# Window attention, forward and backward: two quads in one attention region, with three half sums a pair

## The chip, the cores and the metric

The kernel runs on one NeuronCore of a Trainium2 chip. The metric is the device time of one execution in microseconds. Every product runs on TensorE (PE), which writes PSUM, eight banks of 2 KB per partition; VectorE (DVE) and ScalarE (ACT) copy PSUM to SBUF and do the softmax; SyncE (SP) and GpSimd (POOL) issue the DMAs.

## The reference

The image has 256 x 256 positions and 384 channels in bf16, cut into 1024 windows of 8 x 8 positions. For each window, attention with one head, and then its gradients for a given `grad_out`:

```python
qkv = xw @ wqkv                      # xw: 64 tokens x 384 of one window
q, k, v = split(qkv)
p = softmax(q @ k.T * 384 ** -0.5)
o = (p @ v) @ wo
...
_out, _vjp = jax.vjp(_f, x, wqkv, wo)
return (out, *_vjp(grad_out))        # out, dx, dwqkv, dwo
```

The outputs are `out_0` = o and `out_1` = dx (both 256 x 256 x 384), `out_2` = dwqkv and `out_3` = dwo.

## The kernel before

**Products folded.** At the start the kernel builds A = wq wk' x scale and B = wv wo, and their transposes, 384 x 384 each. A window then needs only z (from grad_out by B', `project` kind 0), y (from x by A, kind 1), u (x by B) and v (x by A', `uv`), and not q, k and v by themselves. The weight gradients come at the end from two 384 x 384 sums over all windows, U'x and W'x, which are gathered in `GF_acc`.

**Tiling.** A *quad* is four pairs of windows: 8 windows, 512 tokens, a tile of 128 partitions x 4 x 384. There are 128 quads, numbered from 0. Quad i passes through: DMA loads of `xq` and `dq` (`load`, L133); their DMA transposes `xT` and `dT` (`load_turn`, L141); z and y into `yz` (`project`, L161); copies into `zy` (`gather`, L175, DVE) and a DMA transpose into `tok` (`to_tokens`, L181); scores into one PSUM bank `sd` (`scores`, L186: P's logits in one half of the partitions and their gradient in the other); the softmax and its gradient (`soft`, steps 0 to 5, DVE except for the exponential); transposes of the two 64 x 64 blocks on DVE (`turn`); u and v (`uv`, L233); and attention (`attend`, L268, once for each of the four window pairs).

**Two forms of matmul.** z, y, u, v, the scores and the row sums use the whole 128 x 128 array, through `product` (all recorded on L157). `attend` works in four tiles of 64 x 64: each `slot` (L277, its products recorded on L283) is four products of 64 rows, for `pw`, `pu`, `po` and `pd`, and the banks go out by `W` (ACT), `U` (DVE), `o` (ACT) and `d` (ACT or DVE, by the table `EV`).

**Sums for the weight gradients.** Three finished quads form a group (GQ = 3). Each group gives six pieces of work (2 sums x 3 row blocks), kept in `fill`. A piece is done in one of two forms: `gf_rows`, 12 products of 128 x 384 into one bank `pg` and one add into `GF_acc`; or `gf_halves`, 12 slots of four 64 x 64-tile products into two banks `ph` and two adds, the second after the first (L320).

**The order of the work** is written out by hand; each engine runs its queue in that order. `step` (L360) handles three quads at once: c (attention), b (scores, softmax, u, v) and a (z, y of the next). Its PE order is: scores of b; u and v of b; z and y of a; one row sum; then `attention` of c, where each of the four `attend` calls is followed by four slots of one half sum until its twelve are done. One row sum and one half sum a quad use up six pieces in three quads.

**PSUM.** All banks come from one pool `ring` of eight. A new tile gets a bank that the program has given back, and its first product waits for the copy (or add) that emptied it.

Of the kernel before, what the change touches and what calls it, by code (L numbers as in the profile page):

```python
# [11 lines left out]
BF16 = mybir.dt.bfloat16  # L12
F32 = mybir.dt.float32

P = 128
WIN = 8
WT = WIN * WIN
QUAD = 4
# [5 lines left out]
def kernel(  # L24
# [21 lines left out]
    nc = tc.nc  # L46
    _, H, W, C = x.shape
    CK = C // P
# [5 lines left out]
    grp = ctx.enter_context(tc.tile_pool(name="grp", bufs=2 * GQ + 1))  # L54
    qp = ctx.enter_context(tc.tile_pool(name="qp", bufs=2))
# [64 lines left out]
    OTHER = {0: HI, WT: LO}  # L120

    def load_first(st):
        st["xq"] = xq = grp.tile([P, QUAD, C], BF16, tag="xq", name="xq", bufs=2 * GQ + 5)
# [9 lines left out]
    def load(st):  # L133
        st["xq"] = xq = grp.tile([P, QUAD, C], BF16, tag="xq", name="xq", bufs=2 * GQ + 5)
        st["dq"] = dq = qp.tile([P, QUAD, C], BF16, tag="dq", name="dq", bufs=6)
        for t in range(QUAD):
            nc.gpsimd.dma_start(out=dq[:, t, :], in_=windows(grad_out, st, 2 * t))  # L137
        for t in range(QUAD):
            (nc.gpsimd if st["i"] == AHEAD + 1 else nc.sync).dma_start(out=xq[:, t, :], in_=windows(x, st, 2 * t))

    def load_turn(st):  # L141
        st["xT"] = qp.tile([P, QUAD, CK, P], BF16, tag="xT", name="xT", bufs=3)
        st["dT"] = qp.tile([P, QUAD, CK, P], BF16, tag="dT", name="dT")
        for src, dst, on_pe in (("dq", "dT", G_ON_PE), ("xq", "xT", X_ON_PE)):
            if st["i"] >= on_pe:
                nc.sync.dma_start_transpose(out=st[dst][:].rearrange("p t m k -> p (t m) k"),
                                            in_=st[src][:].rearrange("p t c -> p (t c)"))

    def turn_on_pe(st, src, dst):
        for t in range(QUAD):  # L150
# [117 lines left out]
    def attend(st, t):  # L268
        if t == 0:
            st["Uq"] = grp.tile([P, QUAD, C], BF16, tag="Uq", name="Uq")  # L270
            st["Wq"] = grp.tile([P, QUAD, C], BF16, tag="Wq", name="Wq")
        copies = {"A": nc.scalar.copy, "D": nc.vector.tensor_copy}

        def bank(name):
            return ring.tile([P, C], F32, tag="r", name=name)

        def slot(bank, straight, crossed, start=False, stop=False):  # L277
            for h in (LO, HI):
                o = OTHER[h.start]
                products = [(h, bank, straight, {"start": True, "stop": True}),  # L280
                            (o, pd[h is LO], crossed, {"start": start, "stop": stop})]
                for o, dst, (lhs, rhs), flags in products if h == LO else products[::-1]:
                    nc.tensor.matmul(dst[o, :], lhsT=operand(st, lhs, t, h), rhs=operand(st, rhs, t, h), **flags)  # L283

        def keep(name, src, i, rows=slice(0, P), sb=None):
            sb = ob.tile([P, C], BF16, tag=name, name=name) if sb is None else sb
            copies[EV[name][i]](out=sb[rows, :], in_=src[rows, :])  # L287
# [6 lines left out]
        copies[EV["W"][t] if st["i"] >= GQ else "DA"[t % 2]](out=st["Wq"][:, t, :], in_=pw[:])  # L294
        pu = bank("pu")
        slot(pu, ("ST", "xq"), ("dS", "y"))
        copies[EV["U"][t]](out=st["Uq"][:, t, :], in_=pu[:])  # L297
        po = bank("po")
        slot(po, ("PT", "uq"), ("ST", "vq"), stop=True)
        o = keep("o", po, t)  # L300
        above, below = rim.pop("d", None) if t == 0 else None, st["at"][0] + 2 * WIN * QUAD < H
        d = keep("d", pd[1], t, slice(0 if t else WT, P), above)
        nc.gpsimd.dma_start(out=windows(out_0, st, 2 * t), in_=o)  # L303
        if t or above is not None:
            nc.gpsimd.dma_start(out=windows(out_1, st, 2 * t - 1), in_=d if t else above[:])  # L305
        else:
            nc.gpsimd.dma_start(out=windows(out_1, st, 0, 1), in_=d)
        if t == QUAD - 1:
            rim["d"] = sb = ob.tile([P, C], BF16, tag="d", name="d")
            keep("d", pd[0], QUAD, LO, sb)  # L310
            if not below:
                nc.gpsimd.dma_start(out=windows(out_1, st, 2 * QUAD - 1, 1), in_=rim.pop("d")[LO, :])

    fill, rim = [], {}
# [34 lines left out]
                nc.vector.tensor_copy(out=final[f][:, ma, :], in_=GF_acc[:, f, ma, :])  # L349
                yield  # L350

    def attention(st):
        halves = gf_halves(*fill.pop(0)) if fill else iter(())
        for t in range(QUAD):
            attend(st, t)
            yield
            for k in range(QUAD):
                next(halves, None)

    def step(c, b, a, ahead):  # L360

# [40 lines left out]
        for rest in slots:  # L402
            pass

    G_ON_PE, X_ON_PE = 2, 1
    EV = {"z": "AAA", "y": "AAA", "u": "AAAA", "v": "AAAA", "o": "AAAA", "U": "DDDD", "W": "AAAA", "d": "DADAA"}
    quads = [(row, col) for col in range(0, W, WIN) for row in range(0, H, 2 * WIN * QUAD)]
    n = len(quads)
    sts = [{"at": q, "i": i, "on_pe": i <= GQ or i == n - 1} for i, q in enumerate(quads)]
# [4 lines left out]
    def weight_gradients(group):  # L414
# [19 lines left out]
                copy_out(k, out, pe[:])  # L434

        def rows(name):
            return grp.tile([P, CK, C], BF16, tag="xq", name=name, bufs=2 * GQ + 5)

        for i in range(CK):
            next(group)  # L440
# [26 lines left out]
    with tc.manual_schedule(engines=MANUAL):  # L467
        spare = sm.tile([P, 1], BF16, name="spare", bufs=1)
        fetch_weights()
        warm_up(7)  # L470
        make_identity(nc, ident[:])
        nc.gpsimd.memset(GF_acc[:], 0.0)
        load_first(sts[0])
        load(sts[1])
        load(sts[2])
        load_turn(sts[0])
        load_turn(sts[1])
# [19 lines left out]
        last = None  # L497
        get = lambda i: sts[i] if 0 <= i < n else None
        for i in range(n + 1):
            if 0 <= i < n - 2:  # L500
                load_turn(sts[i + 2])
            if 0 <= i < n:
                to_tokens(sts[i])
            step(get(i - 1), get(i), get(i + 1), get(i + AHEAD) if i else None)
            if i > 0:
                held.append(sts[i - 1])
                sts[i - 1] = None
            if held and i == n:
                last = gf_final(held)
            elif len(held) == GQ:  # L510
                fill.extend((held, f, ma) for f in range(2) for ma in range(CK))
                held = []
        while fill:
            gf_rows(*fill.pop(0))
        weight_gradients(last)
# [30 lines left out]
```

## Time and profile before

| what | value |
|---|---|
| median of 3 runs | 1897.86 us (1897.47 to 1898.12) |
| the profiled execution | 1897.33 us, of which its span 1895.6 us |
| granted TensorE clock | 1.00 from 300 to 1800 us |
| PE busy from 300 to 1800 us | 1500.00 of 1500.00 us |
| DVE, ACT, POOL busy in that time | 1334.00, 1218.28, 691.54 us |
| u and v products, z, y | 333.6 + 333.4, 269.6, 269.5 us |
| row sums pg, half sums ph | 181.6 + 94.8, 204.2 + 103.4 us |
| adds into GF_acc from ph, from pg | 138.1 us (250, 552 ns each), 74.1 us (133) |
| DMA transposes, median to landing | xT 7.7, dT 7.7, tok 7.4 us |

The span runs from the first to the last instruction of the profiled execution; the rest of its time lies around it. Matmuls are pipelined: an instruction lasts longer than the distance to the next one, so distances between starts are what counts. The same holds for copies on DVE and ACT.

### The profile page before, as it was taken

The numbers are of one execution on the slowest core, as the hardware profiler recorded it, in microseconds if no ns is written. First come the engines' busy times: TensorE is split into PE (matmuls) and PEld (weight loads), VectorE is DVE, ScalarE is ACT, GpSimd is POOL, SyncE is SP. The second block draws the span as 40 slices with busy tenths as digits, with TensorE's granted clock in tenths as the row PEclk, the third lists the DMA queues.
The fourth block names the chain that finished last, engine by engine and source line by source line (L and its number), as shares of the span: only waits on it lengthen the run. The fifth ranks groups of instructions, "written<-read, shape, count | busy, mean of one in ns | idle before, by whom it ended". The sixth has DMA issues, their size and how long they took to land.

```text
span 1895.6 us, 57194 instructions
## 1 busy us (share of the span) xinstructions
PE 1887.7 (100%) x22398; PEld 1125.4 (59%) x22398; DVE 1662.8 (88%) x3602; ACT 1523.7 (80%) x3346; POOL 862.6 (46%) x1576
## 2 busy tenths in 40 slices
PE   9999999999999999999999999999999999999999
PEld 5555565556555655565556555655565566556655
DVE  6888888888888888888888888888888888888887
ACT  7888788878887888788878887888788878887884
POOL 4444444445444444454445444544444445444532
PEclk9999999999999999999999999999999999999999
DMA  9999999999999999999999999999999999999995
GB/s 224 244 212 225 221 211 221 216 221 218 210 222 220 212 224 213 224 215 215 227 215 220 213 218 223 218 208 222 218 222 218 214 222 219 212 213 227 219 183 115
DMA packets 948911, 408.28 MB, mean 215 GB/s; under 512 B 830880, under 2 KB 924064, under 8 KB 948640
## 3 DMA queue, kind: packets, MB, share of 16 engines
q1 hardware_dynamic: 872128, 252.63, 78.2%
q0 software_dynamic: 75264, 151.11, 31.3%
q8 instruction: 175, 2.87, 0.6%
q10 hardware_dynamic: 1248, 0.89, 0.2%
q14 instruction: 96, 0.79, 0.1%
HBM read 101.84 MB, written 101.84 MB: 107 GB/s over the span
## 4 chain that ended last, share of the span: by engine, by line
PE 99%; DVE 1%; ACT 0%; issue 0%; ACTq 0%
PE pj L157 53%; PE pg L157 13%; PE ph L338 13%; PE sd L157 5%; PE pw L283 5%; PE po L283 4%; PE pu L283 4%; PE pd L283 1%; PE pe L427 0%; DVE Uq L297 0%; PE warm L87 0%; PE pc L106 0%; DVE Wq L294 0%; PE pt L99 0%; DVE d L287 0%
## 5 line engine op out<-in xcount | busy, mean ns | idle before, releaser
L303 POOL DMA_DIRECT2D out_dram<-o x512 | 273.6, 534 | 919.3 <-ACT o L287 903.7
L294 ACT CAST Wq<-pw 128x384 bf16<-128x384 f32 x506 | 243.4, 481 | 275.8 <-PE pw L283 275.5
L157 PEld LDWEIGHTS <-xT 128*128 128x128 bf16 x3072 | 291.4, 98 | 182.5
L157 PE MATMUL pj<-B_sb,xT 128*128 128x384 bf16 x1536 | 333.6, 326 | 0.0
L157 PE MATMUL pj<-AT_sb,xT 128*128 128x384 bf16 x1536 | 333.4, 326 | 0.0
L137 POOL DMA_DIRECT2D dq<-in_grad_out_dram x508 | 268.8, 540 | 77.9 <-DMA out_dram<-d 25.2
L297 DVE CAST Uq<-pu 128x384 bf16<-128x384 f32 x512 | 282.8, 552 | 13.8 <-PE pu L283 1.4
L305 POOL DMA_DIRECT2D out_dram<-d x480 | 278.6, 580 | 12.3 <-ACT uq L241 5.1
L157 PE MATMUL pj<-dT,BT_sb 128*128 128x512 bf16 x1152 | 269.6, 379 | 0.1
L157 PE MATMUL pj<-xT,A_sb 128*128 128x512 bf16 x1152 | 269.5, 379 | 0.0
L171 ACT CAST yz<-pj 128x512 bf16<-128x512 f32 x384 | 224.3, 585 | 38.4 <-PE pj L157 29.6
L283 PE MATMUL pd<-tok,ps 64*64 64x384 bf16 x2048 | 254.4, 326 | 0.0
L287 ACT CAST o<-po 128x384 bf16<-128x384 f32 x512 | 250.0, 488 | 1.5 <-PE po L283 1.4
L241 ACT CAST vq<-pj 128x384 bf16<-128x384 f32 x512 | 246.6, 482 | 3.6
L241 ACT CAST uq<-pj 128x384 bf16<-128x384 f32 x512 | 243.7, 476 | 3.7 <-PE pj L157 1.9
L173 ACT CAST yz<-pj 128x512 bf16<-128x512 f32 x384 | 224.7, 585 | 24.5 <-PE pj L157 0.6
L258 DVE STREAM_TRANSPOSE PS<-ps 32x256 bf16<-32x256 bf16 x492 | 214.5, 436 | 9.4
L157 PEld LDWEIGHTS <-xq 128*128 128x128 bf16 x1572 | 153.4, 98 | 115.6 <-issue 0.9
L338 PEld LDWEIGHTS <-xq 64*64 64x64 bf16 x6000 | 175.9, 107 | 67.8
L338 PE MATMUL ph<-Wq,xq 64*64 64x384 bf16 x3984 | 204.2, 323 | 0.0
L157 PEld LDWEIGHTS <-A_sb 128*128 128x128 bf16 x1152 | 112.5, 98 | 135.6
L157 PEld LDWEIGHTS <-BT_sb 128*128 128x128 bf16 x1152 | 112.5, 98 | 122.5
(95 smaller groups left out, 3049.2 us busy)
## 6 DMA issues: line engine op xcount, KB each, us to landing
out_dram<-o POOLq DMA_DIRECT2D x512, 96.0 KB, 3.8
xq<-in_x_dram SPq DMA_DIRECT2D x508, 96.0 KB, 4.0
dq<-in_grad_out_dram POOLq DMA_DIRECT2D x508, 96.0 KB, 5.8
out_dram<-d POOLq DMA_DIRECT2D x480, 96.0 KB, 4.3
out_dram<-d POOLq DMA_DIRECT2D x64, 48.0 KB, 4.8
tok<-zy SPq DMA_TRANSPOSE x128, 7.4
xT<-xq SPq DMA_TRANSPOSE x127, 7.7
dT<-dq SPq DMA_TRANSPOSE x126, 7.7
```

What stands on the lines that cost most here:

```text
L137: nc.gpsimd.dma_start(out=dq[:, t, :], in_=windows(grad_out, st, 2 * t))
L157: nc.tensor.matmul(out, lhsT=lhsT, rhs=rhs, start=start, stop=stop)
L171: ENG[EV["z"][mo]](out=yz[:, mo, :, 0:4:3, :], in_=pj[:])
L173: ENG[EV["y"][mo]](out=yz[:, mo, :, 1:3, :], in_=pj[:])
L241: cp(out=dst[:, t, :], in_=pj[:])
L283: nc.tensor.matmul(dst[o, :], lhsT=operand(st, lhs, t, h), rhs=operand(st, rhs, t, h), **flags)
L287: copies[EV[name][i]](out=sb[rows, :], in_=src[rows, :])
L294: copies[EV["W"][t] if st["i"] >= GQ else "DA"[t % 2]](out=st["Wq"][:, t, :], in_=pw[:])
L297: copies[EV["U"][t]](out=st["Uq"][:, t, :], in_=pu[:])
L303: nc.gpsimd.dma_start(out=windows(out_0, st, 2 * t), in_=o)
L305: nc.gpsimd.dma_start(out=windows(out_1, st, 2 * t - 1), in_=d if t else above[:])
L338: nc.tensor.matmul(dst[o, :], lhsT=st["xq"][h, t, ma * P + o.start:ma * P + o.stop], rhs=st["UW"[f] + "q"][h, t, :], start=(i == 0), stop= ...
```

## The change

From quad 10 on (`PAIRED`), quads are handled two at a time by `double`: first `front` of the even quad i and of the odd quad i + 1, and then both attentions one behind the other. `front(b, a, ...)` has the scores and the softmax of b, z and y of the next quad a, now ahead of u and v of b, and in the even front one row sum ahead of z. In the attention of the even quad two half sums run, six slots behind each `attend`; in that of the odd quad one, four slots behind each. So a pair has one row sum and three half sums where two steps had two and two. The gathers of quad i + 2 stand in the even quad's attention, those of i + 1 in the even front. In the even quad one more of the five `d` copies is ACT's (`EVEN`, from quad 12 on). The loads of x and grad_out and the two transposes are separate calls at other places, `xq` has twelve buffers in place of eleven, and the last quad's blocks are turned on DVE and not on PE. Quads 0 to 9 stay as they were, except that quad 9's attention follows quad 8's and holds no sums.

```diff
-    def attention(st):
-        halves = gf_halves(*fill.pop(0)) if fill else iter(())
+    def attention(st, sets=1):
+        halves = [gf_halves(*fill.pop(0)) for k in range(min(sets, len(fill)))]
+        slots = (None for part in halves for slot in part)
         for t in range(QUAD):
             attend(st, t)
             yield
-            for k in range(QUAD):
-                next(halves, None)
+            for k in range(QUAD if sets < 2 else QUAD + 2):
+                next(slots, None)
+
+    def front(b, a, rows, gathers):
+        scores(b)
+        soft(b, 0)
+        if rows and fill:
+            soft(b, 1)
+            soft(b, 2)
+            for row in range(rows):
+                gf_rows(*fill.pop(0))
+            z = 0
+        else:
+            z = 2
+            for mo in range(z if a is not None else 0):
+                project(a, 0, mo)
+            soft(b, 1)
+            soft(b, 2)
+        i = b["i"]
+        if a is not None:
+            for mo in range(z, CK):
+                project(a, 0, mo)
+        soft(b, 3)
+        soft(b, 4)
+        soft(b, 5)
+        if i % 2 == 0 and i + AHEAD < n:
+            load_xq(sts[i + AHEAD])
+        if i + AHEAD < n:
+            load_dq(sts[i + AHEAD])
+        if i + 3 < n:
+            load_turn(sts[i + 3], "dT")
+        if a is not None:
+            for mo in range(CK):
+                project(a, 1, mo)
+        if gathers and a is not None:
+            for kind in range(2):
+                gather(a, kind)
+            to_tokens(a)
+        turn(b)
+        if i % 2 == 0 and i + AHEAD + 1 < n:
+            load_xq(sts[i + AHEAD + 1])
+        for t in range(QUAD):
+            for part in range(2):
+                uv(b, t, part)
+        if i + 3 < n:
+            load_turn(sts[i + 3], "xT")
+
+    def double(i):
+        a = sts[i + 2] if i + 2 < n else None
+        front(sts[i], sts[i + 1], EVEN_ROWS, True)
+        front(sts[i + 1], a, ODD_ROWS if a is not None else 2, False)
+        for t, part in enumerate(attention(sts[i], EVEN_SETS)):
+            if t >= 2 and a is not None:
+                gather(a, t - 2)
+        if a is not None:
+            to_tokens(a)
+        for part in attention(sts[i + 1]):
+            pass
...
+            ev = EVEN if st["i"] > PAIRED and st["i"] % 2 == 0 and name in EVEN else EV
+            copies[ev[name][i]](out=sb[rows, :], in_=src[rows, :])
...
+    EVEN_ROWS, ODD_ROWS, EVEN_SETS = 1, 0, 2
+    PAIRED = 10
     EV = {"z": "AAA", "y": "AAA", "u": "AAAA", "v": "AAAA", "o": "AAAA", "U": "DDDD", "W": "AAAA", "d": "DADAA"}
+    EVEN = {"d": "AADAA"}
...
+        for i in range(PAIRED, n, 2):
+            double(i)
+            done(sts[i], sts[i + 1])
+        last = gf_final(held)
```

More of the change, by code (lines that the diff above doesn't have):

```diff
@@ L122, in load_first @@
     def load_first(st):
-        st["xq"] = xq = grp.tile([P, QUAD, C], BF16, tag="xq", name="xq", bufs=2 * GQ + 5)
+        st["xq"] = xq = grp.tile([P, QUAD, C], BF16, tag="xq", name="xq", bufs=2 * GQ + 6)
         st["dq"] = dq = qp.tile([P, QUAD, C], BF16, tag="dq", name="dq", bufs=6)
@@ L131, in load_first, with load_dq @@
         nc.gpsimd.tensor_copy(out=spare[:], in_=dq[:, QUAD - 1, 0:1])
-    def load(st):
-        st["xq"] = xq = grp.tile([P, QUAD, C], BF16, tag="xq", name="xq", bufs=2 * GQ + 5)
+    def load_dq(st):
         st["dq"] = dq = qp.tile([P, QUAD, C], BF16, tag="dq", name="dq", bufs=6)
@@ L137, in load, with load_xq, load_turn @@
             nc.gpsimd.dma_start(out=dq[:, t, :], in_=windows(grad_out, st, 2 * t))
+    def load_xq(st):
+        st["xq"] = xq = grp.tile([P, QUAD, C], BF16, tag="xq", name="xq", bufs=2 * GQ + 6)
         for t in range(QUAD):
             (nc.gpsimd if st["i"] == AHEAD + 1 else nc.sync).dma_start(out=xq[:, t, :], in_=windows(x, st, 2 * t))
[L141 to L147, printed above, removed]
+    def load(st):
+        load_dq(st)
+        load_xq(st)
+    def load_turn(st, dst):
+        st[dst] = qp.tile([P, QUAD, CK, P], BF16, tag=dst, name=dst, bufs={"xT": 3, "dT": 2}[dst])
+        if st["i"] >= ON_PE[dst]:
+            nc.sync.dma_start_transpose(out=st[dst][:].rearrange("p t m k -> p (t m) k"),
+                                        in_=st[dst[0] + "q"][:].rearrange("p t c -> p (t c)"))
     def turn_on_pe(st, src, dst):
@@ L286, in keep @@
             sb = ob.tile([P, C], BF16, tag=name, name=name) if sb is None else sb
-            copies[EV[name][i]](out=sb[rows, :], in_=src[rows, :])
+            ev = EVEN if st["i"] > PAIRED and st["i"] % 2 == 0 and name in EVEN else EV
+            copies[ev[name][i]](out=sb[rows, :], in_=src[rows, :])
             return sb[rows, :]
@@ L403, in step @@
             pass
-    G_ON_PE, X_ON_PE = 2, 1
+    ON_PE = {"dT": 2, "xT": 1}
+    EVEN_ROWS, ODD_ROWS, EVEN_SETS = 1, 0, 2
+    PAIRED = 10
     EV = {"z": "AAA", "y": "AAA", "u": "AAAA", "v": "AAAA", "o": "AAAA", "U": "DDDD", "W": "AAAA", "d": "DADAA"}
+    EVEN = {"d": "AADAA"}
     quads = [(row, col) for col in range(0, W, WIN) for row in range(0, H, 2 * WIN * QUAD)]
     n = len(quads)
-    sts = [{"at": q, "i": i, "on_pe": i <= GQ or i == n - 1} for i, q in enumerate(quads)]
+    sts = [{"at": q, "i": i, "on_pe": i <= GQ} for i, q in enumerate(quads)]
     AHEAD = 4
@@ L436, in rows @@
         def rows(name):
-            return grp.tile([P, CK, C], BF16, tag="xq", name=name, bufs=2 * GQ + 5)
+            return grp.tile([P, CK, C], BF16, tag="xq", name=name, bufs=2 * GQ + 6)
         for i in range(CK):
@@ L475 @@
         load(sts[2])
-        load_turn(sts[0])
-        load_turn(sts[1])
+        for st in sts[:2]:
+            for dst in ("dT", "xT"):
+                load_turn(st, dst)
         load(sts[3])
@@ L496, with done @@
         held = []
-        last = None
         get = lambda i: sts[i] if 0 <= i < n else None
[L499 to L503, printed above, removed]
-            step(get(i - 1), get(i), get(i + 1), get(i + AHEAD) if i else None)
[L505 to L512, printed above, removed]
+        def done(*quads):
+            for st in quads:
+                held.append(st)
+                sts[st["i"]] = None
+                if len(held) == GQ:
+                    group = held[:]
+                    fill.extend((group, f, ma) for f in range(2) for ma in range(CK))
+                    held.clear()
+        for i in range(PAIRED):
+            for dst in ("dT", "xT"):
+                load_turn(sts[i + 2], dst)
+            to_tokens(sts[i])
+            step(get(i - 1), get(i), get(i + 1), get(i + AHEAD) if i else None)
+            if i > 0 and i < PAIRED - 1:
+                done(sts[i - 1])
+        for dst in ("dT", "xT"):
+            load_turn(sts[PAIRED + 2], dst)
+        to_tokens(sts[PAIRED])
+        for part in attention(sts[PAIRED - 1]):
+            pass
+        done(sts[PAIRED - 2], sts[PAIRED - 1])
+        for i in range(PAIRED, n, 2):
+            double(i)
+            done(sts[i], sts[i + 1])
+        last = gf_final(held)
         while fill:
```

## The prediction

> **What bounds the kernel now.** I read the page's busy shares and chain first, then what TensorE (PE) waits for, then the timeline of one steady step, engine by engine.
>
> ```profile
> PE 1887.7 (100%) x22398; PEld 1125.4 (59%) x22398; DVE 1662.8 (88%) x3602; ACT 1523.7 (80%) x3346; POOL 862.6 (46%) x1576
> ...
> PE 99%; DVE 1%; ACT 0%; issue 0%; ACTq 0%
> ```
>
> PE is 99% of the chain. The waits of PE are four rows, all early:
>
> ```profile
> PE po L283 <- DVE Wq L294: 1.2, 3, 0.4
> PE pw L283 <- DVE Uq L297: 0.7, 3, 0.2
> ```
>
> So what PE does between its products is all that can be saved. The timeline of PE shows it:
>
> ```profile
> 1005.73 2.11 PE L157 MATMUL pg<-Uq,xq 128*128 128x384 bf16 x12
> 1007.77 0.35 PE L283 MATMUL pw<-dq,ps 64*64 64x384 bf16 x1
> ...
> 1008.29 0.82 PE L338 MATMUL ph<-Wq,xq 64*64 64x384 bf16 x16
> 1008.94 0.32 PE L283 MATMUL pw<-dq,ps 64*64 64x384 bf16 x1
> ...
> 1011.54 0.32 PE L283 MATMUL po<-uq,PS 64*64 64x384 bf16 x1
> ...
> 1011.80 0.87 PE L157 MATMUL sd<-xT,yz 128*128 128x64 bf16 x24
> ```
>
> Three things are read here. (1) 128x384 products start 0.1625 us apart (three take 0.4875 in the rows of u and v, 1012.51 to 1013.00); twelve of pg from 1005.73 end at 1007.68, but pw starts at 1007.77: going into the 64-row tiles costs 0.09. The last po slot would be followed at 1011.70, but sd starts at 1011.80: going back costs 0.10. **Together 0.195 us per quad is all the idle time PE has.** (2) Sixteen half products (four slots) take 0.65, so a slot is 0.1625 and twelve are 1.95: a half sum costs PE what a row sum costs. (3) An attend call (pw, pu, po) is 0.49.
>
> VectorE (DVE) empties PSUM banks in the same stretch:
>
> ```profile
> 1007.88 0.56 DVE L320 TENSOR_TENSOR GF_acc<-pg,GF_acc 128x384 f32<-128x384 f32 x1 [0.45 <-PE pg L157]
> 1008.36 0.55 DVE L297 CAST Uq<-pu 128x384 bf16<-128x384 f32 x1
> 1008.94 0.56 DVE L287 CAST d<-pd 64x384 bf16<-64x384 f32 x1
> 1009.53 0.56 DVE L297 CAST Uq<-pu 128x384 bf16<-128x384 f32 x1
> 1010.00 0.55 DVE L179 COPY zy<-yz 128x1536 bf16<-128x1536 bf16 x1
> 1010.62 0.56 DVE L297 CAST Uq<-pu 128x384 bf16<-128x384 f32 x1
> 1011.10 0.55 DVE L287 CAST d<-pd 128x384 bf16<-128x384 f32 x1
> 1011.56 1.14 DVE L320 TENSOR_TENSOR GF_acc<-ph,GF_acc 128x384 f32<-128x384 f32 x2
> 1012.62 0.55 DVE L297 CAST Uq<-pu 128x384 bf16<-128x384 f32 x1
> ...
> 1022.45 0.56 DVE L320 TENSOR_TENSOR GF_acc<-pg,GF_acc 128x384 f32<-128x384 f32 x1 [0.44 <-PE pg L157]
> ```
>
> The pg adds give the period, 14.57 a quad. Full-width copies start 0.475 apart though each lasts 0.555; beside a 64-partition copy, and between the two adds of one half sum, it is 0.58. ScalarE (ACT) starts copies 0.375 apart, each lasting 0.48:
>
> ```profile
> 1011.60 0.48 ACT L294 CAST Wq<-pw 128x384 bf16<-128x384 f32 x1 [0.27 <-PE pw L283]
> 1011.97 0.48 ACT L287 CAST o<-po 128x384 bf16<-128x384 f32 x1
> 1012.34 0.86 ACT L287 CAST d<-pd 128x384 bf16<-128x384 f32 x2
> ```
>
> A product is readable 0.37 to 0.38 after its last instruction starts (pg's last at 1007.52, its add at 1007.88; pw 1008.94, its W copy 1009.32). At 39.29 PE goes on 0.05 after the copy that it waited for ends. So **a bank is back 0.60 after its DVE copy starts, 0.54 after an ACT copy.**
>
> **The change, part by part.** A pair of quads has one attention region, so two mode changes where it had four: it saves 0.195. One row sum becomes a half sum: nothing on PE by (2). z and y go ahead of u and v, which changes no product. There are 59 pairs (quads 10 to 127), so without new waits it would save 59 x 0.195 = 11.5 us.
>
> What it adds are waits for banks. The eight banks go round in order of release; I followed each PE wait of the built program to the copy that it names. With T = 0 at the even quad's first pw (attends at 0, 1.50, 2.96, each followed by six half slots):
> - *First half sum to second.* Its last slot starts at 2.80 and DVE is idle, so its first add runs 3.17 to 3.73 and that bank is back at 3.78. Attend 2 takes PE to 3.45, where the second half sum's second bank must be just that one. **Wait 0.33.** Before, a region held one half sum, and its banks were wanted only in the next stretch.
> - DVE then has: second add 3.75, U2 4.23, d2 4.70, gather 5.17, U3 5.64, gather 6.12. PE ends the second sum's slots at 6.21. Its first add is ready at 6.43, but starts behind the last gather, at 6.59.
> - *Odd quad, first attend* (6.21): the pd bank waits for U3, back at 6.24 (0.03). At 6.73 the third half sum needs the bank of d4, ACT's fourth copy after 5.16, back at 6.81, and the bank of the add that began at 6.59, back at 7.20: **wait 0.48.**
> - DVE goes on: second add 7.17, U0 7.65, d0 8.23 (64 partitions), U1 8.82. PE's second attend starts at 7.85 and its po needs U0's bank (8.25): 0.08; the third's pu needs U1's (9.42): 0.20.
> - The rest just fits: sd follows at 10.98 and needs d2's bank, back at 10.91.
>
> Without waits the region would last 0.52 + 7 x 0.4875 + 36 x 0.1625 + 0.10 = 9.88; the walk gives 10.98, so **1.10 us of waits a pair against 0.195 saved: +0.905 x 59 = +53 us.** All of PE's later work queues behind each wait, and nothing else on PE can be pulled ahead.
>
> By the Trainium skill ("TensorEngine Tiling (Array Packing)", section PSUM Bottleneck) tiling speeds up TensorE but not the emptying of PSUM, so the copies may become the bound. Taken as a rate it would not decide here: the region holds 19 DVE operations, at 0.475 about 9.1 us, and 23 ACT copies, at 0.375 8.6 us, both under 9.88, so by that sum no wait would follow; the trace's bank times above are what I go by.
>
> Edits that I cost at nothing: the fronts. In the even front the row sum (1.95) and z, y (3.88) cover the softmax: DVE leaves the region at 11.9 (last U), so mx to dS, both gathers and the transposes (0.46 + 0.46 + 0.45 + ... as in the rows 1013.20 to 1021.45, 8.2 us with the exp) end about 10.7 after sd, and the odd sd comes at 10.44; the odd front's chain ends 0.6 into the region, where its result is wanted at 6.2. Without this cover each 0.1 costs 6 us. Two copies go from DVE to ACT and one add is new, inside the walk. On SP's queue the transposes stand in a new order; a quad's issues (dT 1.9 to 3.4, xT 3.4, tok 4.6 to 5.9, four xq 2.5 to 3.1 in the rows from 997 to 1029) fill most of 14.57, but each transposition can be issued 16 us or more ahead of its use and lands 7.4 to 7.7 later (medians of the DMA rows). POOL's queue passes 17 outputs at 0.52 in the region (8.9 us) and then eight dq loads, wanted a pair later. The twelfth xq buffer costs only memory. Once each: quad 9's attention without half sums is paced by 11 ACT copies (about +1.5); the last quad's 16 PE transposes go, and two row sums fill the wait of the end (1876.5 to 1879.1 in the chain), about -1.
>
> **Sum.** The profiled run took 1897.33 (span 1895.6 and 1.7 around it); +53.4 and +0.5 give **1951 us**. The median shown, 1897.86, is 0.5 above that run.
>
> **The rivals.**
> - *Stall-free, faster:* if the adds and U copies brought the banks back before the slots need them, the mode changes alone would count: 1897.3 - 11.5 = **1886**. It decides at the first add: it would have to free its bank 0.33 earlier than 0.37 + 0.56 + 0.05 after the last slot. For it: PE never waits today. Against: those three terms are rows of today's trace. Chance 0.05.
> - *Only the two waits for adds:* if gathers and U copies are not in the way (add ready 6.43, back at 7.04, 0.31), waits are 0.64: +0.445 x 59 = 26, **1924**. Chance 0.16.
> - *DVE falls further behind:* the trace doesn't show what follows a gather. At 0.58 in place of 0.475 behind both, and 0.58 ahead of d2, all odd waits come about 0.3 later, 1.45 in all: +74, **1972**. The same size follows if a transposition comes late. Chance 0.14.
> - *PE's clock falls:* granted clock was 1.00 from 30 to 70 us, where PE also waited. The seven warm-up products at 1.19 to 4.19 started 0.43 apart, twice the 0.2155 of z; a region at that pace would add 9.9 x 59 = 584, **2481**. The Trainium skill ("TensorE: Matmul & The Clock Gate", A second HAM failure mode: psum-queue depth-cycling) tells of a kernel whose clock swung through such short idles; the rows of 30 to 70 us don't show it. Chance 0.01.
> - *It doesn't do what it says:* the built program has one 64-tile region a pair with three half sums, and one row sum. Nothing is left for this.
>
> **How the numbers follow.** Forecast 0.62 (within 15 us of 1951), and 0.02 that waits and savings balance near 1897. Range 1921 to 1975: from the two-waits case to the late-DVE case, with 3 us on each side. Faster 0.05, within 0.2% (about what can be told from no change) 0.02, slower 0.93.
>
> **What would show it.** PE's waits should list ph <- DVE GF_acc about 118 times at 0.33 to 0.5, some 45 us, and smaller ones for pd, po and pu <- DVE Uq, some 18 us; sd of even quads 30.0 apart. No wait on GF_acc proves me wrong; so does a gap between po and pw of two quads of a pair, or a clock below 1.00.

## The result, and the profile after

The changed kernel takes **2005.46 us** (median of 5 runs, 1999.14 to 2015.07), the kernel before 1898.12 us (1897.47 to 1899.43): ratio 1.0566, 95% interval 1.0530 to 1.0601. The forecast was 1951 us with a range of 1921 to 1975. It is slower, as forecast, but by twice as much, and the time is outside the range. The profiled execution, the fastest of the five, took 1999.14 us (span 1997.4).

First the page of the changed kernel: engines, busy rows of DMA, the two large queues, the chain.

```profile
PE 1929.9 (97%) x24470; PEld 1182.9 (59%) x24470; DVE 1647.8 (82%) x3607; ACT 1568.8 (79%) x3403; POOL 841.8 (42%) x1576
...
q1 hardware_dynamic: 872128, 252.63, 82.2%
q0 software_dynamic: 75264, 151.11, 31.4%
...
PE 72%; DMA 21%; DVE 5%; issue 1%; ACT 0%; SPq 0%; DVEq 0%; ACTq 0%
PE pj L161 42%; DMA tok<-zy 19%; PE ph L343 9%; PE pg L161 7%; PE sd L161 4%; PE pd L287 3%; DMA xT<-xq 2%; PE pu L287 2%; PE po L287 2%; PE pw L287 2%; DVE Uq L302 1%; DVE GF_acc L325 1%; DVE zy L183 1%; DVE d L292 1%; PE pe L492 0%
```

Before, 99% of the chain was PE. Now 21% is DMA, nearly all of it one transposition, tok. Packets and megabytes of both queues are those of before; only the time that the packets took has grown (q1 was 78.2%, q0 31.3%). What PE waits for (us in total, times, longest):

```profile
PE pd L287 <- DMA tok<-zy: 49.5, 35, 4.2
PE ph L343 <- DVE GF_acc L325: 2.2, 13, 0.2
PE pj L161 <- DMA xT<-xq: 1.8, 3, 1.1
```

The bank waits that the forecast is made of are in no such row, and yet they are there: a half product's record lasts 0.32 us while the next starts 0.16 later, so a wait below about 0.3 us hides under the record before it. It shows only in the distance between starts. PE's timeline of a pair that waits for no DMA, some rows of it (the odd quad's attention begins at 954.27):

```profile
929.16 0.87 PE L161 MATMUL sd<-xT,yz 128*128 128x64 bf16 x24
...
939.60 0.86 PE L161 MATMUL sd<-xT,yz 128*128 128x64 bf16 x24
...
948.18 0.35 PE L287 MATMUL pw<-dq,ps 64*64 64x384 bf16 x1
...
951.62 1.51 PE L343 MATMUL ph<-Uq,xq 64*64 64x384 bf16 x24
952.81 0.32 PE L287 MATMUL pw<-dq,ps 64*64 64x384 bf16 x1
...
954.27 0.32 PE L287 MATMUL pw<-dq,ps 64*64 64x384 bf16 x1
...
954.99 1.21 PE L343 MATMUL ph<-Uq,xq 64*64 64x384 bf16 x16
955.87 0.32 PE L287 MATMUL pw<-dq,ps 64*64 64x384 bf16 x1
...
956.41 0.32 PE L287 MATMUL po<-uq,PS 64*64 64x384 bf16 x1
...
957.59 0.32 PE L287 MATMUL pu<-xq,PS 64*64 64x384 bf16 x1
...
959.18 0.87 PE L161 MATMUL sd<-xT,yz 128*128 128x64 bf16 x24
```

From even sd to odd sd 10.44, from even sd to the next even sd 30.02: the forecast had 10.44 and 30.04. In 31 of 57 pairs it is 30.02 to 30.1; the mean is 30.84 and the longest 36.1. So the time of this execution has two parts: (30.02 - 29.14) x 59 = 52 us in every pair, and (30.84 - 30.02) x 57 = 47 us in the pairs in which tok is late. The second part is not in the forecast.

The first part is the forecast's. These copies and adds of the same region give back the banks that PE waits for:

```profile
951.35 1.15 DVE L325 TENSOR_TENSOR GF_acc<-ph,GF_acc 128x384 f32<-128x384 f32 x2 [0.58 <-PE ph L343]
...
954.74 1.15 DVE L325 TENSOR_TENSOR GF_acc<-ph,GF_acc 128x384 f32<-128x384 f32 x2
955.81 0.55 DVE L302 CAST Uq<-pu 128x384 bf16<-128x384 f32 x1
...
956.98 0.56 DVE L302 CAST Uq<-pu 128x384 bf16<-128x384 f32 x1
```

```profile
954.08 0.85 ACT L292 CAST d<-pd 128x384 bf16<-128x384 f32 x2
```

ACT's second copy of d ends at 954.93 and the third half sum starts at 954.99; U0's copy ends at 956.36 and po starts at 956.41; U1's ends at 957.54 and pu starts at 957.59. PE goes on 0.05 to 0.06 behind each copy, as the prediction read it at 39.29, and the trace's semaphores name the same copies. Counted from the even quad's first pw (948.18), with 0.05 behind the end of the two adds:

| bank given back by | forecast | here |
|---|---|---|
| first add of the first half sum (begins 951.35, lasts 0.56) | 3.78 | 3.78 |
| ACT's second copy of d (d4 of the forecast) | 6.81 | 6.81 |
| first add of the second half sum (begins 954.74, lasts 0.56) | 7.20 | 7.17 |
| U0 | 8.25 | 8.23 |
| U1 | 9.42 | 9.41 |
| sd of the next even quad starts | 10.98 | 11.00 |

Where the second part comes from shows on SP's queue, in the same pair:

```profile
938.91 2.53 SPq L141 DMA_DIRECT2D xq<-in_x_dram  x4
941.67 4.45 SPq L150 DMA_TRANSPOSE dT<-dq  x1
946.21 3.91 SPq L187 DMA_TRANSPOSE tok<-zy  x1
```

The tok of the odd quad is issued at 946.21, 17.05 us after the even sd; its gather had ended some 8 us after it. SP's rows follow one another without a break, and it gets to this tok some 9 us after the gather. This tok lands 24.5 us after the even sd, and the odd attention wants it at 25.1 (954.27): 0.6 us of slack. POOL's queue of that pair:

```profile
933.19 0.53 POOL L310 DMA_DIRECT2D out_dram<-d  x1 [2.56 <-ACT ex L216]
933.72 0.57 POOL L317 DMA_DIRECT2D out_dram<-d  x1
934.29 4.70 POOL L136 DMA_DIRECT2D dq<-in_grad_out_dram  x8
949.83 0.55 POOL L308 DMA_DIRECT2D out_dram<-o  x1 [10.84 <-ACT o L292]
```

Eight grad_out loads go out in one piece right behind the copies out of two attentions. And the DMA rows (last column: median us from issue to landing; before, out o 3.8, dq 5.8, tok 7.4):

```profile
out_dram<-o POOLq DMA_DIRECT2D x512, 96.0 KB, 4.6
...
dq<-in_grad_out_dram POOLq DMA_DIRECT2D x508, 96.0 KB, 7.8
...
tok<-zy SPq DMA_TRANSPOSE x128, 9.1
```

### The profile page after: what moved, and what is told of

Its sections match the earlier page's. It is cut to its first block, busy times and chain, and to the rows that moved or that the text cites. A ratio compares the mean times of both kernels' runs of the same rounds, so it can differ in the third digit from the quotient of the medians.

```text
span 1997.4 us, 61289 instructions
## 1 busy us (share of the span) xinstructions
PE 1929.9 (97%) x24470; PEld 1182.9 (59%) x24470; DVE 1647.8 (82%) x3607; ACT 1568.8 (79%) x3403; POOL 841.8 (42%) x1576
## 4 chain that ended last, share of the span: by engine, by line
PE 72%; DMA 21%; DVE 5%; issue 1%; ACT 0%; SPq 0%; DVEq 0%; ACTq 0%
PE pj L161 42%; DMA tok<-zy 19%; PE ph L343 9%; PE pg L161 7%; PE sd L161 4%; PE pd L287 3%; DMA xT<-xq 2%; PE pu L287 2%; PE po L287 2%; PE pw L287 2%; DVE Uq L302 1%; DVE GF_acc L325 1%; DVE zy L183 1%; DVE d L292 1%; PE pe L492 0%
## 5 line engine op out<-in xcount | busy, mean ns | idle before, releaser
L161 PEld LDWEIGHTS <-xT 128*128 128x128 bf16 x3072 | 299.9, 98 | 209.8
L343 PEld LDWEIGHTS <-xq 64*64 64x64 bf16 x8784 | 307.4, 107 | 100.8 <-issue 35.2
L136 POOL DMA_DIRECT2D dq<-in_grad_out_dram x508 | 273.7, 548 | 160.6 <-DMA out_dram<-d 71.9
L287 PE MATMUL pd<-tok,ps 64*64 64x384 bf16 x2048 | 265.7, 329 | 52.4 <-DMA tok<-zy 49.5
L310 POOL DMA_DIRECT2D out_dram<-d x480 | 256.9, 535 | 88.8 <-DVE d L292 49.0
L343 PE MATMUL ph<-Wq,xq 64*64 64x384 bf16 x4848 | 267.5, 326 | 2.0 <-DVE GF_acc L325 0.7
L325 DVE TENSOR_TENSOR GF_acc<-ph,GF_acc 128x384 f32<-128x384 f32 x366 | 203.3, 556 | 40.5 <-PE ph L343 34.2
L287 PE MATMUL pw<-dq,ps 64*64 64x384 bf16 x1024 | 221.9, 329 | 0.8 <-DVE Uq L302 0.7
L343 PE MATMUL ph<-Uq,xq 64*64 64x384 bf16 x3936 | 217.1, 323 | 2.7 <-DVE GF_acc L325 1.5
```

Source lines behind the costliest of these rows:

```text
L161: nc.tensor.matmul(out, lhsT=lhsT, rhs=rhs, start=start, stop=stop)
L325: nc.vector.tensor_tensor(out=GF_acc[:, f, ma, :], in0=pw[:], in1=GF_acc[:, f, ma, :], op=ALU.add)
L343: nc.tensor.matmul(dst[o, :], lhsT=st["xq"][h, t, ma * P + o.start:ma * P + o.stop], rhs=st["UW"[f] + "q"][h, t, :], start=(i == 0), stop= ...
```

## The experiments

The theories, as they came up. **S**: tok stands in the wrong place on SP's queue. **D**: in the order of the pairs the DMA engines need more than 30.02 us a pair, so whatever PE gains comes back as a wait for tok. Within D, why: **R**, the amount of traffic; **M**, copies and transpositions side by side; **P**, the long burst on POOL's queue; **Q**, the order on SP's queue; **E**, the engines' own work. **H**: not the pace but a late start that is never made up. Against all of them stands the forecast's theory that the loss is bank waits; that is part of the loss in each.

### 1. Place on SP's queue, and two row sums

```diff
 e1_tok_first
-        if i + 3 < n:
-            load_turn(sts[i + 3], "dT")
...
             to_tokens(a)
+        if i + 3 < n:
+            load_turn(sts[i + 3], "dT")
```

> The changed kernel with one move on SP's queue: in front, the transposition of dT(i+3) is issued behind that of tok(i+1) and not ahead of it. Theory S (place in SP's queue): tok is late because it stands behind a transposition that nobody needs for another pair; the 52 us of waits for tok go, the pair settles at 30.0 us, and the time is 1951 us, within 8. Theory D (the DMA engines' rate: they are busy all the time and need about 30.5 us a pair): the waits for tok get a little shorter or move to another tile, and the time stays between 1980 and 2010.

Measured 2007.08 us (2003.66 to 2016.77), ratio 1.0581 (1.0553 to 1.0608). S falls: the place ahead of one dT is not it. The waits for xT grew instead (18.9 us).

```diff
 e2_rows
-    EVEN_ROWS, ODD_ROWS, EVEN_SETS = 1, 0, 2
+    EVEN_ROWS, ODD_ROWS, EVEN_SETS = 1, 1, 1
```

> The changed kernel with two row sums and two half sums a pair (EVEN_ROWS, ODD_ROWS, EVEN_SETS = 1, 1, 1), so that no half sum needs the bank of the one before it within a region. Theory of bank waits (both S and D): PE's waits for banks, 1.1 us a pair in the changed kernel, fall under 0.3. Then S: the pair is 29.0 to 29.3 plus the same waits for tok (some 50 us in all), 1930 to 1950 us. D: what PE gains it gives back as waits for tok, 1985 to 2010 us with waits for tok over 90 us.

> Both edits: two row sums and two half sums a pair, and tok(i+1) ahead of dT(i+3) on SP's queue. S: 1885 to 1900 us, near or below the kernel before. D: 1980 to 2005 us, as without either edit.

e2_rows: 2024.32 us, ratio 1.0666 (1.0628 to 1.0704); e3_rows_tok, both edits: 2015.74 us, ratio 1.0618 (1.0588 to 1.0648). Both are above all ranges named. A miss: I took it that a half sum fewer in the region takes bank waits away. It adds some. PE's waits in e3_rows_tok:

```profile
PE pd L287 <- DVE GF_acc L325: 37.2, 56, 0.7
PE pu L287 <- DVE GF_acc L325: 13.4, 56, 0.2
PE pd L287 <- DMA tok<-zy: 7.3, 5, 3.2
```

With fewer half products between them the attends follow closer, and the first of the odd quad waits for the adds: the shortest pair is 30.82, not 30.02. D had expected over 90 us of waits for tok; in e2_rows 16.4 us are left and in e3_rows_tok 7.3, since PE by itself now takes as long as the DMAs (30.90 us in most pairs, beside the pace of about 30.8 found in section 7). That fits D, but the forecast of it was wrong.

### 2. Relief for the DMA engines

```diff
 e4_no_out0
-        nc.gpsimd.dma_start(out=windows(out_0, st, 2 * t), in_=o)
+        if st["i"] < PAIRED:
+            nc.gpsimd.dma_start(out=windows(out_0, st, 2 * t), in_=o)
```

> The changed kernel without the DMA writes of out_0 from quad 10 on (that output is left unwritten there; all copies on the engines stay). It takes a quarter of POOL's DMA traffic away and nothing from SP's queue. D: SP's transposes are issued and land sooner, the waits for tok go, and the time is 1951 us, within 8. S: the order on SP's queue is the same, tok is as late as before, 1985 to 2010 us.

Measured 1953.22 us (1952.10 to 1953.46), ratio 1.0287 (1.0272 to 1.0303); every pair takes 30.02, and tok's waits shrink to one:

```profile
PE pd L287 <- DMA tok<-zy: 2.4, 1, 2.4
PE po L287 <- DVE Wq L299: 1.2, 3, 0.4
```

The control is the kernel before with the same relief:

```diff
 e12_before_no_out0
-        nc.gpsimd.dma_start(out=windows(out_0, st, 2 * t), in_=o)
+        if st["i"] < 10:
+            nc.gpsimd.dma_start(out=windows(out_0, st, 2 * t), in_=o)
```

> Left out: out_0 is not written from the eleventh quad on. The kernel before with the relief of e4_no_out0. Theory D (the changed kernel alone is bound by DMA, the one before by PE): 1893 to 1899, no gain. If the missing copies help PE, ACT or POOL by themselves: the same 45 to 55 us less as in the changed kernel, about 1845.

1897.83 us (one run): no gain. The copies matter to the paired order alone, and the 0.88 us a pair that is left is PE's own. D holds.

### 3. One part of the change alone

The kernel before with its step reordered: soft 1 and 2, the row sum, z, soft 3 to 5, y, and then all of u and v.

```diff
 e8_zy_first
-        B(uv, 0, 0)
-        B(uv, 0, 1)
         B(soft, 1)
...
         for mo in range(CK):
             A(project, 1, mo)
-        for rows in range(1 if a is not None else 2):
-            if fill:
-                gf_rows(*fill.pop(0))
+        for t in range(QUAD):
+            for part in range(2):
+                B(uv, t, part)
```

> The kernel before with one part of the change alone: z and y products and the row sum ahead of the u and v products, no quads paired. PE's work is the same, DMA orders on SP and POOL are the same as before. If the loss is in the pairing (bank waits 0.9 us and DMA 0.8 us a pair): 1885 to 1910. If the order of the products by itself makes the transpositions late (theory Z): 1930 or more.

1901.11 us, ratio 1.0018 (1.0008 to 1.0028). z and y ahead of u and v cost next to nothing; the loss is in the pairing.

### 4. Are the bank waits the gathers' doing?

```diff
 e10_gather_no_out0 (with the edit of e4_no_out0)
-            if t >= 2 and a is not None:
-                gather(a, t - 2)
+            if t < 2 and a is not None:
+                gather(a, t)
```

> Left out: out_0 is not written from the eleventh quad on, as in e4_no_out0, so that the DMA engines do not hide what PE does (there every pair took 30.02 us). On top, the two gathers of quad i+2 run on VectorE after windows 0 and 1 of the even attention, not 2 and 3. Bank-wait theory of the prediction (a pair's 0.9 us over two quads of before are waits of PE for banks that VectorE's queue frees late; two gathers of 0.47 us stand ahead of the adds at 25.6 and 26.2 us): the pair falls by 0.3 to 0.9 us, to 29.1 to 29.7, the run to 1900 to 1934 us. If the 0.9 us are something else on PE (modes, issue): 30.02 and 1951.

Every pair but the first takes 29.92, 0.10 less; the one run 1953.25 us (at its start one wait of 7 us for tok took back what 59 x 0.10 gave). Less than the 0.3 to 0.9 expected: the wait of the third half sum falls from 0.24 to 0.13, and all others stay. So the gathers are a small part; the walk itself had given them no more than 0.16 (an add ready at 6.43 that begins at 6.59), and the range named here asked too much of them. With the whole traffic, and the loads of e6_dq_sp below, e11_gather_dq_sp:

> The changed kernel whole, with the gathers moved as in e10_gather_no_out0 and the grad_out loads on SP's queue as in e6_dq_sp (1980 us). If the DMA engines' pace is the bound (theory D), PE's faster pair is not seen: 1970 to 1990. If the PE time saved is added to what DMA leaves: 1930 to 1955.

1982.80 us (1975.72 to 1987.85), beside e6's 1980.32: nothing of PE's gain is seen, as D says.

### 5. The DMA traffic by itself

e5_streams has no computation, only the DMAs of 20 pairs a stage, held in step by the loads that the transpositions read.

```diff
 e5_streams, the two orders
+    SP = {"quads": (("xq", 0), ("dT", 0), ("xT", 0), ("tok", 0), ("xq", 1), ("dT", 1), ("xT", 1), ("tok", 1)),
+          "pairs": (("xq", 0), ("dT", 0), ("tok", 0), ("xq", 1), ("xT", 0), ("dT", 1), ("xT", 1), ("tok", 1))}
+    POOL = {"quads": (("dq", 0), ("outs", 0), ("dq", 1), ("outs", 1)),
+            "pairs": (("outs", 0), ("outs", 1), ("dq", 0), ("dq", 1))}
```

> Left out: all computation; the outputs hold no results. Only the DMA traffic of the kernels is run, in four stages of 20 pairs of quads: (1) SP's queue alone: 8 x copies and 6 transpositions a pair, (2) POOL's queue alone: 8 copies in and 16 out a pair, (3) both, in the order of the kernel before (per quad 4 + 8 copies beside x, dT, xT, tok), (4) both, in the order of the changed kernel (16 copies out, then 8 in, beside its own order of transpositions). Estimates from rows: transpositions run at 960 packets a us in the quiet stretches of the profile of before, so 12250 packets take 12.8 us a pair, and the x copies some 5 more: stage 1 about 18 us a pair; POOL issues a copy in 0.53 us: stage 2 about 12.7 to 14. Theory M (copies of POOL's queue and transpositions that run side by side slow each other, so the order decides): stage 3 at most 29.1, stage 4 30 to 31.5. Rival R (a pair's traffic takes the 16 engines the same time in any order): stages 3 and 4 within 0.3 us of each other.

> Left out: all computation; the outputs hold no results. DMA traffic alone again, four stages of 20 pairs of quads; e5_streams measured SP's queue alone 20.5 us a pair, POOL's alone 12.7, both in the order of before 25.2, both in the order of the change 27.4. Here: (1) SP's queue alone in the order of the change, (2) SP in the order of before beside POOL in that of the change (16 out, 8 in), (3) SP in the order of the change beside POOL in that of before, (4) SP in the order of the change with the grad_out loads on SP, POOL with the copies out alone. Theory P (the long burst on POOL's queue costs the 2.2 us): stage 2 about 27.4, stage 3 about 25.2. Theory Q (the order on SP's queue costs it): stage 2 about 25.2, stage 3 about 27.4. Stage 1: 20.5 by either. Stage 4, from e6_dq_sp's gain of 25 us over 59 pairs (0.4 us a pair): about 27.0 or less.

> Left out: all computation of the reference; the outputs hold no results. The DMA traffic in the order of the change (e5_streams: 27.3 us a pair) in four stages of 20 pairs: (1) alone, (2) beside TensorE at work without a break (384-column products), (3) beside ScalarE and VectorE at work without a break (copies of 128x384 from PSUM), (4) beside all three. If the engines' work slows the DMA (theory E): stage 4 at 30 us a pair or more, and stage 2 or 3 shows which engine. If not: 27.3 in all four within 0.7, and what the kernel adds is in its order of waits, which the stages do not have.

One run of each kernel. Mean us a pair, between landings of the last tok of a pair, without the first two and the last of each stage (the 25.2 and 27.4 named above are the same two stages with one pair more left out):

| on SP's queue | on POOL's queue | us a pair |
|---|---|---|
| order of before | nothing | 20.55 |
| order of the change | nothing | 20.58 |
| nothing | order of before | 12.75 |
| order of before | order of before | 25.58 |
| order of before | order of the change | 27.91 |
| order of the change | order of before | 26.04 |
| order of the change | order of the change | 27.31, again 27.45 |
| order of the change, and the grad_out loads | copies out alone | 30.10 |

The same traffic takes 1.3 to 2.3 us longer a pair when POOL's queue has it as 16 copies out and then 8 in; the order on SP's queue moves it by about 0.5 one way or the other. R falls and Q falls, P holds.

It is not that SP waits longer for the loads that dT reads: in the two stages with 16 out and then 8 in, dT waits 1.06 and 0.87 us a pair for POOL's queue, in the two with the order of before 2.75 and 1.37.

The levels missed: I expected stage 1 at 18, the stage in the order of the change above 30, and the last row at 27.0 or less, where it is 30.10. That last stage differs in one thing more, since its copies out wait for the xT of their own pair. The kernel with these loads on SP's queue got faster (e6 below), the stage slower: levels of the stages can't be carried over to the kernel.

In the last of these kernels, e18_streams_busy, beside TensorE, beside ScalarE and VectorE, and beside all three, each busy for 94 to 95% of the stage, the stages took 27.78, 27.76 and 27.93: E falls. What lifts 27.3 to 30.8 in the kernel is not among the stages; they lack the kernel's waits.

### 6. Copies moved from POOL's queue to SP's

```diff
 e6_dq_sp
-            nc.gpsimd.dma_start(out=dq[:, t, :], in_=windows(grad_out, st, 2 * t))
+            (nc.sync if st["i"] > PAIRED + AHEAD else nc.gpsimd).dma_start(out=dq[:, t, :], in_=windows(grad_out, st, 2 * t))
 e7_out1_sp
-            nc.gpsimd.dma_start(out=windows(out_1, st, 2 * t - 1), in_=d if t else above[:])
+            (nc.sync if st["i"] > PAIRED else nc.gpsimd).dma_start(out=windows(out_1, st, 2 * t - 1), in_=d if t else above[:])
```

> The grad_out loads of the paired quads go through SP's queue, ahead of the same queue's transpositions, and no longer run beside them from POOL's queue. The traffic is the same. Theory M: fewer transpositions meet copies, the pair comes down towards the walk's 30.02 us: 1951 to 1985 us. Rival R (the amount of traffic alone counts): 1995 to 2015. Rival I (SP's time to issue is what is short; eight more issues of 0.5 to 0.7 us a pair, 4 to 5.5 us): above 2030.

> Most out_1 copies of the paired quads go through SP's queue in place of POOL's: half of the burst of copies out can then not run beside transpositions. Same traffic. Theory M: 1951 to 1985. Rival R: 1995 to 2015. Rival I, or SP held up behind copies that wait for the attention: above 2015.

e6: 1980.32 us (1979.72 to 1988.54), ratio 1.0439 (1.0413 to 1.0465), 25 us less than the change; its pairs take 30.46 on the mean. That lies in M's range; section 8 shows that M is not the reason. e7: one run of 1963.71 us, in whose trace 56 of 57 pairs take 30.02, and three of 2016 to 2028, of which there is no trace. What sets them apart is not shown; that the program keeps step in one run and not in the others was the guess that raised H.

### 7. Is it the pace, or a late start?

```diff
 e13_pause12 (e14_pause24: 112; e16_pause_mid: 112 at i == 68; e15_out1_pause: 56, on e7_out1_sp)
+            if i == 12:
+                pause(56)
             double(i)
```

`pause(n)` puts n idle products of 512 columns on PE, once.

> The changed kernel with 56 idle products of 512 columns (0.216 us each, from nine z products in 1.94 us: 12.1 us) once on PE, ahead of the second pair, so that SP can catch up with the 9 us it is behind. Work added: 12 us. Theory H (in step it stays in step): 1951 + 12 = 1963 us, within 5. Rival D (the DMA pace of the paired order is above 30.02 us a pair, the lead is used up): a lead of 10 to 12 us is gone after some 15 pairs, 2003 to 2015.

> The same with 112 products, 24.2 us. Theory H: 1951 + 24 = 1975 us, within 5. Rival D: 2003 to 2020. If 12 us are too few for SP to come into step and 24 are enough, this run alone shows H.

> e7_out1_sp (most out_1 copies on SP's queue: one run of 1964 us with every pair at 30.02, the others 2016 to 2028) with the pause of 12.1 us ahead of the second pair. Theory H: all runs at 1963 to 1975. Rival D: most runs at 2016 to 2040 as before.

> The changed kernel with the pause of 24.2 us ahead of the thirtieth pair, the middle of the paired part. Theory H: the pairs before it as in the changed kernel (mean 30.8), those after it 30.02: 2005 + 24 - 24 = about 2003 us. Rival D: after some pairs at 30.02 back to 30.8 and more: 2015 to 2029. The trace tells more than the time.

e13: 2007.22 us (1997.94 to 2019.91). e14: 2053.09 (2034.88 to 2063.59). e16: 2026.30 (2016.41 to 2039.13). H falls, for the changed order: the pause puts SP in step (in e13 tok of the odd quad is issued 7.9 us after the even sd, in the pair before 19.8), the next 11 or 12 pairs take 30.02, and then the waits are back. PE's waits for tok in e13, from 230 to 590 us and from 590 to 950 us:

```profile
PE pd L293 <- DMA tok<-zy: 2.6, 1, 2.6
```

```profile
PE pd L293 <- DMA tok<-zy: 16.5, 6, 4.5
```

A lead of 9 to 10 us lasts 12 pairs: 0.8 us a pair, so the DMA pace in this order is about 30.8 us. Once the lead is gone, pairs take 31.1 on the mean in e13, 31.7 in e14 and 32.0 in e16, worse than the 30.8 of the change, and e14's time is above what D expected; the cause of that stays open. e15: 1976.33 us (1968.24 to 1982.44), 51 of 57 pairs at 30.02: with the out_1 copies on SP's queue a lead lasts nearly the whole run, so the pace there is near 30.02. The times lie between the ranges of H and D.

### 8. The burst taken apart

The grad_out loads of each quad are held on POOL until the first u product of that quad is copied; nothing else differs.

```diff
 e17_dq_spread
-        if i + AHEAD < n:
-            load_dq(sts[i + AHEAD])
...
             for part in range(2):
                 uv(b, t, part)
+            if t == 0 and i + AHEAD < n:
+                nc.gpsimd.tensor_copy(out=spare[:], in_=b["uq"][:, 0, 0:1])
+                load_dq(sts[i + AHEAD])
```

> The changed kernel with the grad_out loads of each quad held on POOL until the first u product of that quad is copied (about 7.6 and 18 us into the pair), by a copy of one column ahead of them on POOL. They no longer follow the 16 copies out in one burst of 24, but fall into the stretch in which POOL's queue is quiet now. Same traffic. Theory P (the long burst costs): nearer the walk, 1951 to 1985. Theory M (what costs is copies beside transpositions, and the quiet stretch is what the transpositions need): 2005 to 2040. Rival R (amount of traffic alone): 1995 to 2010.

**1952.59 us** (1951.94 to 1953.99), ratio 1.0288 (1.0271 to 1.0305): 52.9 us less than the change, with all of its traffic. POOL's queue in one pair, even sd at 907.45:

```profile
912.01 0.57 POOL L317 DMA_DIRECT2D out_dram<-d  x1
915.35 0.19 POOL L406 COPY spare<-uq 128x1 bf16<-128x1 bf16 x1 [2.76 <-ACT uq L245]
915.94 2.11 POOL L136 DMA_DIRECT2D dq<-in_grad_out_dram  x4 [0.41 <-PE pj L161]
924.11 0.35 POOL L406 COPY spare<-uq 128x1 bf16<-128x1 bf16 x1 [6.06 <-ACT uq L245]
924.67 2.09 POOL L136 DMA_DIRECT2D dq<-in_grad_out_dram  x4 [0.20 <-PE pj L161]
928.12 0.55 POOL L308 DMA_DIRECT2D out_dram<-o  x1 [1.35 <-ACT o L292]
```

Within the pair the first four loads go 3.4 us later than in the change (8.5 us after the even sd, for 5.1), the other four some 10 us later (17.2, for 7.6). On SP's queue tok follows its gather at once, 8.0 us after the even sd:

```profile
912.61 2.10 SPq L150 DMA_TRANSPOSE dT<-dq  x1
915.44 4.19 SPq L187 DMA_TRANSPOSE tok<-zy  x1
```

All 57 pairs take 30.02. The run enters the paired part nearly as late as the change does (tok of the odd quad issued 16.0 us after the even sd in the first pair, 17.8 in the change) and needs no pause: within seven pairs it is in step. So the pace is now below 30.02, where it was 30.8. The chain of its page, and PE's wait for tok:

```profile
PE 85%; DVE 11%; DMA 2%; issue 2%; ACT 0%; SPq 0%; DVEq 0%; POOL 0%; ACTq 0%
```

```profile
PE pd L287 <- DMA tok<-zy: 0.3, 1, 0.3
```

M said slower, for the loads now run beside transpositions that had POOL's queue quiet before: M falls, and so does R. That the order of copies on POOL's queue costs the 52.9 us is shown; whether it is the length of the burst, as P has it, or the moment at which the loads go is not, since e17 changes both. A hint for the length, from one run: in the trace of e7, with half as many copies out on POOL's queue, the eight loads go in one piece and no later than in the change, and the pairs take 30.02. None of these versions beats the kernel before; the best is this one, slower by the 0.88 us a pair that is PE's own.

## Why the prediction was wrong

- *Mode changes, half sum equal to row sum:* borne out in the sums. The row sum takes 1.95 (929.87 to 931.82 in the timeline) and leads into z without a mode change, where it took 2.04 before the region.
- *The walk of the banks, 1.10 us a pair, +53 us:* right, and in its parts. Pairs of 30.02 against 30.04, and 1952.59 (e17) and 1953.22 us (e4) against 1951; each bank that PE waits for comes back within 0.03 us of the forecast (the table behind the result). What differs is how the waits share the 1.1. The second half sum loses 0.22 (951.62 to 952.81 is 1.19, for 0.975) and not 0.33, so PE comes to the odd quad 0.12 earlier. There it loses 0.46 for d's bank and the add's together (954.27 to 955.87 is 1.60, for 0.49 and 0.65; forecast 0.51), and 0.21 each for U0 and U1 (forecast 0.08 and 0.20). The sum stays the same because VectorE, busy without a break from 951.35 to 957.54, sets when U0 and U1 give their banks back, whenever PE comes to ask for them.
- **The step that failed** is the cover given to the DMAs: "each transposition can be issued 16 us or more ahead of its use and lands 7.4 to 7.7 later", and "POOL's queue passes 17 outputs at 0.52 in the region (8.9 us) and then eight dq loads, wanted a pair later". Both were costed at nothing. The burst was seen, and asked only whether its own loads come too late. They don't; what they hold up is SP's transpositions on the same engines. By e17 that costs 52.9 us. The 16 us ahead were a place in the program; SP, busy without a break, got there 9 us late.
- What could have been read before: the page of before had the DMA row at 9 throughout, packet times of 1.12 to 1.13 of the 16 engines' span from 300 to 1800 us, and SP's issues filling most of the step. The forecast names the last and stops there. The row by itself decides nothing: from 300 to 1800 us packet times are 1.10 to 1.15 in e17, where PE does not wait, and 1.16 to 1.18 in the change. But with such a row the question is not whether one transfer has slack, but whether the pair's traffic still fits in the new order.
- *The rival "DVE falls further behind", 1972, with "a late transposition" as an afterthought:* DVE did not fall behind. The late transposition should have been a rival of its own, with the DMA pace as its price.
- *Stall-free (1886) and two waits (1924):* not so; 30.02 in e4 and e17 excludes both.
- *"A clock below 1.00" as a sign against:* it was 0.99 to 1.00 in stretches of 300 us, and 1.00 throughout in e17, where PE has no such waits. It goes with the waits. They are 49.5 us long and the loss in those pairs is 47, so it explains no loss of its own.
- *"PE's waits should list ph <- DVE GF_acc about 118 times":* a wrong sign, not a wrong step: waits that short are covered by the records (13 are listed, 2.2 us).

The Trainium skill ("DMA: Bandwidth & Descriptors", Rules for kernel authors) says that spreading DMAs over SP, ACT and GpSimd gives no bandwidth, since all run on the same 16 engines. The streams agree: 20.6 and 12.75 us alone, 25.6 together, not 20.6; SP's waits for POOL's loads are 2.75 of the 5 us between. The same page (Queues, rings and completion order) says that each engine takes turns between queues packet by packet; by that rule a backlog of POOL's large packets slows SP's small ones for as long as it lasts, which fits e17, but no run here shows the turns. (By the q0 and q1 rows, POOL's packets hold 2.0 KB on the mean and SP's 0.29 KB.)

## What to carry to other kernels

When the DMA engines are busy throughout, cost a reordering also by what each queue will hold in one piece: ask for whom a burst is in the way, not only whether it comes in time itself. A queue whose issuer is never idle has no slack that a program order could show; compare its issue times with its semaphores. And short waits of PE are read from distances between starts, since the list of waits leaves them out.

## What the runs showed of the hardware

- The same DMAs take 25.6 or 27.9 us a pair by the order of copies on POOL's queue alone, with SP's order the same. Why that order costs it inside the engines stays open, and so does the step from 27.3 us for the traffic alone to 30.8 in the kernel.
- TensorE, ScalarE and VectorE, busy for 94 to 95% of the time, slow this traffic by 0.5 us a pair at most (27.45 to 27.93).
- PE went on 0.05 to 0.06 us after the copy that freed a PSUM bank ended, in all three waits that the rows show (954.93 to 954.99, 956.36 to 956.41, 957.54 to 957.59).
- Holding a load back made the whole faster: grad_out loads sent 3.4 and 10 us later landed 5.7 us after issue (median) and not 7.8, and the transpositions dT and xT took 5.3 and 5.7 where they had taken 7.0 and 7.7.
